# A third shifted copy made by two DMAs instead of VectorE, in a mixed attention and MLP kernel

## The chip, the cores and the metric

The kernel runs on one core of a Trainium2 chip. The metric is the device time of one execution in microseconds (us). TensorE multiplies matrices, ScalarE evaluates exponentials, VectorE does elementwise work, GpSimd is a further elementwise engine that can also issue DMAs, and SyncE (SP) issues nearly all DMAs. Each engine works through its own list of instructions in the order in which the program wrote them, and waits on semaphores for the others.

## The reference, cut to what matters

The input `x` is 2048 x 640 in bfloat16. It is layer-normed, and goes into two branches: attention with 32 heads of width 20, and an MLP that mixes along the sequence. The output is `x + attention * silu(mlp)`.

```python
xn = layernorm(x)
q, k, v = split_heads(xn @ wqkv)              # 32 heads, 20 wide
p = softmax(q @ k.T * 20 ** -0.5)             # 2048 x 2048 per head
s = merge_heads(p @ v) @ wo
u = gelu(einsum("bsd,sf->bdf", layernorm(xn), w1) + b1)
g = silu(transpose(einsum("bdf,fs->bds", u, w2) + b2))
out = x + s * g
```

Most of the work is in the scores: 32 heads x 4 blocks of 512 queries x 16 blocks of 128 keys make 2048 tiles of 128 x 512, and each needs an exponential and a product with `v`.

## The kernel before

**A planner writes every engine's program.** `Prog` keeps a list of tasks for each engine and a modelled time `T` for each. A task names the slots that it reads and writes; `Prog._add` derives from them the semaphore waits, and a modelled finish `fin`. The class `_Kern` runs a greedy loop over the engines: it asks each what it could do next (`pe_cands`, `eng_cands`), and appends the candidate that can start first. So the order on the chip is the order of the model, fixed when the program is built; on the chip nothing is reordered. DMAs go to SP in the order in which the planner emits them, over eight semaphores in rotation (`Prog.dma`).

**Scores.** Heads are taken in groups of four (`G`), and for each group the queries in blocks of 512 (`p`); a pair (G, p) is a pass `q`. A unit is one tile of scores, for one head and one block of keys. `emit_st` issues the score matmuls for up to four units at once, one in each 32-row part of TensorE (L1283). Two groups of three PSUM banks serve ScalarE, one further bank (`JB`) serves VectorE, and one (`AB`) accumulates the values. `do_st` can lend the last bank of a ScalarE group to VectorE when the modelled load of VectorE (`dve_load`) is below `LEND`.

**ScalarE's tiles.** `emit_exp` takes two or three banks through one activation, exp(scores), into `pt_sb` (L1313).

**VectorE's tiles.** VectorE makes an approximate exponential of the tiles of a *quad*: the four heads of a group for one block of keys. `emit_op1` adds a constant to the scaled scores, cuts at zero and writes the result as uint16 (L1324). These bits, read as bfloat16, are roughly 2 to the power of the score; the mantissa is linear between powers. Four such values, shifted by a quarter of a power each and weighted, average out most of the error. `emit_top` therefore makes three more copies of the finished quad, adding the integer constants `DK = (0, 32, 64, 96)` to the bits, each in one operation over 128 x 2048 elements:

```python
tk = pr.dve(lambda e: e.tensor_scalar(dst, src, dk, None, ALU.add), ...)   # L1362
```

The four versions are k = 0, 1, 2, 3; the first is the quad itself, in buffer `b0`. They live in `dt_sb`, eight buffers (`NTILE`) of 4 x 512 uint16 per partition; `tfree` lists the free ones, and at most three quads (`NLIVE`) are open at once. Only key blocks 0, 3, 6, 9 and 12 (`RC`) may become quads, because these have weighted values `vs_sb`, one set for each k over 0.

**Values.** `emit_pv` multiplies tiles with the values and accumulates (L1381). A ScalarE unit takes one matmul; a quad takes four for each k. Four heads run side by side in column parts of 32. Which of a quad's versions go next, and how many at once, is chosen in `pe_cands` (`PARTS` = (3, 1), or all that are there); a version's buffer goes back to `tfree` after its matmuls. `mk` lets a piece become a candidate 60 ns after the modelled finish of the last version that it reads.

**The rest.** Projections, the MLP and the output products are jobs whose matmuls fill TensorE's time between score groups (L648, L656, L965 and others). Where nothing fits, `emit_fill` issues matmuls with zeros (L1398).

Of the kernel before, what the change touches and what calls it, by code (L numbers as in the profile page):

```python
# [10 lines left out]
P = 128  # L11
# [28 lines left out]
class Prog:  # L40
# [2 lines left out]

    COMPUTE = ("pe", "act", "dve", "pool", "sp")
    LAT = {"pe": 55.0, "act": 55.0, "dve": 55.0, "pool": 80.0, "sp": 60.0}
    TAIL = {"pe": 170.0, "act": 118.0, "dve": 82.0, "pool": 60.0, "sp": 0.0}

    def __init__(self, nc, n_lanes=8):
        self.nc = nc
        self.n_lanes = n_lanes  # L50
        self.cengs = list(self.COMPUTE) + [f"d{i}" for i in range(n_lanes)]
# [8 lines left out]
        self.pipe = 0.0  # L60
        self.pe_end = 0.0
        self.low = 0
        self.lowt = 0.0
        self.alog = []
# [21 lines left out]
    def _add(self, eng, ceng, fn, reads, writes, name, extra_req=(), cost=100.0, tail=None):  # L86
        t = _Task(eng, ceng, fn, name)
        t.gidx = self.gcount
        self.gcount += 1
        self.tasks[eng].append(t)  # L90
        self.ctasks[ceng].append(t)
        t.cidx = len(self.ctasks[ceng])
        req = {}

        def need(tt):
            if tt is None:
                return
            if eng == "pe" and tt.ceng == "pe":
                return
            cur = req.get(tt.ceng)  # L100
            if cur is None or tt.cidx > cur.cidx:
                req[tt.ceng] = tt

        for s in reads:
            assert s.w is not None, f"read of uninit slot {s.name} by {name}"
            need(s.w)
        for s in writes:
            need(s.w)
            for r in s.readers.values():
                if r is not t:  # L110
                    need(r)
        for tt in extra_req:
            need(tt)
        start = self.T[eng]
        for tt in req.values():
            start = max(start, tt.fin + self.lat(eng, tt.ceng))
        kn = list(self.known[eng])
        for tt in sorted(req.values(), key=lambda x: -x.gidx):
            ci = self.cidx_of[tt.ceng]
            if kn[ci] >= tt.cidx:  # L120
                continue
# [12 lines left out]
        for s in writes:  # L134
            s.w = t
            s.readers = {}
        t.t0 = start
        if ceng not in self.COMPUTE:
            start = max(start, 700.0)
            if tail is not None:  # L140
                self.T[eng] = start + cost
                self.pipe = max(self.pipe, start) + cost
                t.fin = self.pipe - cost + tail
            else:
                self.T[eng] = start + 450.0
                self.pipe = max(self.pipe, start + 600.0) + cost
                t.fin = self.pipe + (1200.0 if self.pipe < 2500.0 else 2800.0 if cost > 800.0 else 1400.0)
        else:
            self.T[eng] = start + cost
            self.busy[eng] += cost  # L150
            t.fin = start + cost + (self.TAIL[eng] if tail is None else tail)
        return t
# [31 lines left out]
    def dma(self, fn, reads=(), writes=(), name="dma", lane=None, cost=3000.0, over=(), tail=None):  # L184
# [11 lines left out]
        t.need_inc = True  # L196
        return t

    def final_waits(self):
        for li in range(self.n_lanes):  # L200
            ceng = f"d{li}"
# [9 lines left out]
    def emit(self, sems):  # L211
# [12 lines left out]
        def make(engname):  # L224
            def body(eng):
                for t in self.tasks[engname]:
# [3 lines left out]
                    if t.fn is None:  # L230
                        continue
                    ins = t.fn(eng)
                    if engname == "sp" and t.ceng.startswith("d"):
# [32 lines left out]
class _Kern:  # L266
# [42 lines left out]
    QAT = (0.0, 0.0, 0.0, 0.0)  # L309
    ACTP = 30.0  # L310
    COLS = True
    NTILE, NLIVE, EARLY = 8, 3, True
    QC = ((0.5, 3.0), (3.2, 6.4), (9.0, 13.5), (14.0, 18.0), (19.0, 22.0))
    WIN = 16
    DON = True
    TOPP, EVP = 38.0, 36.0
    GROT = 1
    OPTS = (
        ("SLACK", (120.0, 40.0, 200.0, 320.0)),
        ("MINJ", (640.0, 320.0, 1000.0)),  # L320
        ("ROOM", (3, 6, 0)),
        ("DRIDE", (400.0, 150.0, 700.0)),
        ("LEND", (1800.0, 1300.0, 2400.0, 700.0, 0.0)),
        ("PARTS", ((2,), (2, 1), (3, 1), (1,), ())),
        ("LATE", (2.0, -9.0, 99.0)),
        ("DON", (True, False)),
        ("LONE", (False, True)),
        ("CONFL", (True, False)),
        ("TOPP", (38.0, 22.0)),
        ("EVP", (24.0, 36.0)),  # L330
        ("FGAP", (40.0, 150.0)),
        ("GROT", (1, 0)),
    )
    PLAN = ()
    PARTS = (3, 1)
# [17 lines left out]
    def build(self):  # L353
# [4 lines left out]
        with es:  # L358
# [19 lines left out]
            sb("dt_sb", [P, self.NTILE, 4, 512], u16)  # L378
# [13 lines left out]
            t["ps_all"] = E(nc.psum_tensor("ps_all", [P, 4096], f32))  # L392
            t["qk_dram"] = nc.dram_tensor("qk_scratch_dram", [2, 560, S], bf)
            t["oT_dram"] = nc.dram_tensor("oT_scratch_dram", [8 * P, S], bf)
            t["ok_dram"] = nc.dram_tensor("ok_scratch_dram", [S, 512], bf)
            sems = {}
            for e in ("pe", "act", "dve", "pool", "sp"):
                sems[e] = E(nc.semaphore(f"sem_{e}"))
            for i in range(pr.n_lanes):
                sems[f"d{i}"] = E(nc.semaphore(f"sem_d{i}"))  # L400
            self.t = t
            self.schedule()
            pr.final_waits()
# [7 lines left out]
    def schedule(self):  # L411
# [715 lines left out]
        avail = []  # L1127
        dquads = []
        tfree = list(range(self.NTILE))
        dlive = [0]  # L1130
        dop1 = []
        lent = set()
# [187 lines left out]
        def emit_op1():  # L1320
# [12 lines left out]
            if d["left"] == 0:  # L1333
                dtop.append([d, 1])
                d["fin"][0] = tk.fin
                if self.EARLY:
                    dquads.append((0.0, d))

        def emit_top():
            d, k = dtop[0]  # L1340
# [25 lines left out]
            dtop[0][1] += 1  # L1366
            for j in range(k, k + n):
                d["fin"][j] = tk.fin
            if k + n == 4:
                dtop.pop(0)  # L1370
                if not self.EARLY:
                    dquads.append((tk.fin, d))
                for j in range(2 if n == 2 else 1):
                    if d["pk"] > j:
# [37 lines left out]
        def emit_pv(items, quads):  # L1412
# [5 lines left out]
            freed = []  # L1418
            for d, n_ in quads:
                for k in range(d["pk"], d["pk"] + n_):  # L1420
                    for g in range(4):
                        seq.append(("d", d, k, g))
                    if k > (1 if self.MERGE else 0) or d["tl"][3] is not None:
# [16 lines left out]
            for i, s in enumerate(seq):  # L1440
# [15 lines left out]
                else:  # L1456
# [7 lines left out]
                    pt_busy[s0] = False  # L1464
                    avail.remove((fin, u, s0))
            tfree.extend(freed)
            for d in ends:
                dlive[0] -= 1
                dquads[:] = [x for x in dquads if x[1] is not d]
# [83 lines left out]
        for w in (1, 0):  # L1553
# [2 lines left out]
                       [S_("wkr" if w else "wqr")], f"wr{w}", 491520))  # L1556
        rw.append(("tag", "wr"))
        add_job("wr", rw, ("xTd15",), 30.0)
        add_job("bload", [
            ("dma", small(lambda e: e.dma_start(bload_sb[:, 0:FC], B_b1.rearrange("(fc p) -> p fc", p=P))), [], [S_("bl1")],  # L1560
             "dma_b1", 3000),
# [215 lines left out]
        def pe_cands(T):  # L1777
# [28 lines left out]
            if acc_ok[0] and pv_pass[0] < NP:  # L1806
# [29 lines left out]
                if quads:  # L1836
                    d0 = quads[0][1]
                    have = sum(f > 0.0 for f in d0["fin"])
                    left = have - d0["pk"]
                    whole = have == 4  # L1840
                    if left > 0 and whole:
                        if min(cnt) >= 1 or rem == len(pick):
                            pv.append(mk(pick, [(quads[0], left)]))
                            if len(pick) < rem or not pick:
                                pv.append(mk([], [(quads[0], left)]))
                        else:
                            pv.append(mk([], [(quads[0], left)]))
                    for n in self.PARTS:
                        if n < left or (n == left and not whole):
                            pv.append(mk([], [(quads[0], n)]))  # L1850
                if okp:
                    pv.append(mk(pick, []))
            jb = []
# [332 lines left out]
```

## Time and profile before

| | |
|---|---|
| median of 2 runs | 754.68 us (754.28 to 755.08) |
| the profiled execution, its own time | 754.1 us |
| its span, first to last instruction | 752.3 us |
| TensorE busy | 716.3 us (95%) |
| VectorE busy | 719.0 us (96%) |
| ScalarE busy | 730.0 us (97%) |
| GpSimd busy | 15.3 us (2%) |
| DMA queues, share of 16 engines | 23.4% + 0.8% + 0.1% |

In the profile's lines PE is TensorE (PEld its weight loads), ACT ScalarE, DVE VectorE, POOL GpSimd and SP SyncE; `L12` is a line of the kernel. A group's line gives what it writes and reads, the shape, the count, then the busy time and the mean of one in ns, and then the engine's idle time before these instructions with the engine that ended it. A row of digits shows 40 equal slices of the span, busy tenths in each. In a waits line the three numbers are us in total, times, and the longest. A timeline line starts with the start and the length in us. A windows line has the stretch, its length, the busy time of PE, PEld, DVE, ACT and POOL with counts, the granted clock, the DMA share and GB/s.

### The profile page before, as it was taken

How to read it: one execution, taken by the hardware profiler on the slowest of the kernel's cores; microseconds unless marked ns; L12 is line 12 of the kernel's file. 1: busy time of each engine (PE TensorE's matmuls, PEld its weight loads, DVE VectorE, ACT ScalarE, POOL GpSimd, SP SyncE). 2: the span in 40 equal slices, each digit the busy share in tenths (PEclk: the TensorE clock that was granted, in tenths of full speed). 3: DMA queues.
4: the chain of work that ended last, by engine and by line, in shares of the span. 5: the costliest groups of instructions: out<-in, count | busy, mean ns of one | idle time of the engine just before them, and what ended most of it. 6: DMA issues, size and time to landing. Idle time of an engine off the chain costs nothing.

```text
span 752.3 us, 23672 instructions
## 1 busy us (share of the span) xinstructions
PE 716.3 (95%) x10561; PEld 243.6 (32%) x10561; DVE 719.0 (96%) x1320; ACT 730.0 (97%) x707; POOL 15.3 (2%) x23
## 2 busy tenths in 40 slices
PE   9899999999999999999999999999999999999997
PEld 7332222222233232323223332323233332333233
DVE  7889999999999999999999999999999999999996
ACT  5989999999999999999999999999999999999995
POOL 4200000000000000000000000000000000000000
PEclk9999999999999999999999999999999999999999
DMA  8754111110121031212111131301325501041102
GB/s 237 155 110 48 56 38 37 20 38 5 38 62 20 13 76 31 72 24 69 20 38 21 30 87 24 74 13 29 79 76 81 128 28 51 7 152 47 47 15 70
DMA packets 119738, 42.66 MB, mean 57 GB/s; under 512 B 79172, under 2 KB 118468, under 8 KB 119588
## 3 DMA queue, kind: packets, MB, share of 16 engines
q1 hardware_dynamic: 119636, 41.15, 23.4%
q8 instruction: 82, 1.34, 0.8%
q14 instruction: 20, 0.16, 0.1%
HBM read 26.37 MB, written 10.22 MB: 49 GB/s over the span
## 4 chain that ended last, share of the span: by engine, by line
ACT 76%; PE 18%; DVE 6%; issue 0%; DVEq 0%
ACT pt_sb L1313 74%; PE ps_all L1381 5%; PE ps_all L1283 5%; PE ps_all L648 5%; DVE dt_sb L1324 1%; PE ps_all L1408 1%; ACT zt_sb L849 1%; DVE dt_sb L1362 1%; ACT zt_sb L844 1%; DVE bst_sb L532 1%; DVE bst_sb L530 1%; DVE regC L548 1%; PE ps_all L965 1%; PE ps_all L633 0%; DVE v_sb L1114 0%; PE ps_all L746 0%
## 5 line engine op out<-in xcount | busy, mean ns | idle before, releaser
L1313 ACT ACTIVATE pt_sb<-ps_all 128x1024 bf16<-128x1024 f32 (+1 forms) x681 | 711.2, 1242 | 4.9 <-PE ps_all L1283 2.1
L1324 DVE TENSOR_SCALAR dt_sb<-ps_all 128x512 uint16<-128x512 f32 x496 | 328.4, 683 | 15.9 <-PE ps_all L1283 8.9
L1283 PE MATMUL ps_all<-qk_sb 32*128 32x512 bf16 (+1 forms) x2128 | 269.1, 376 | 26.4 <-ACT pt_sb L1313 22.9
L1362 DVE TENSOR_SCALAR dt_sb<-dt_sb 128x2048 uint16<-128x2048 uint16 x372 | 241.2, 689 | 1.5
L1283 PEld LDWEIGHTS ps_all<-qk_sb 32*128 32x128 bf16 x2128 | 68.4, 91 | 280.9 <-ACT pt_sb L1313 226.4
L1381 PE MATMUL ps_all<-dt_sb,vs_sb 128*21 128x512 bf16 (+1 forms) x1536 | 130.7, 376 | 0.9 <-DVE dt_sb L1362 0.5
L1381 PE MATMUL ps_all<-pt_sb,v_sb 128*21 128x512 bf16 (+1 forms) x1616 | 127.0, 374 | 1.9 <-DVE v_sb L1114 0.9
L648 PE MATMUL ps_all<-regC,regA 128*32 128x128 bf16 (+1 forms) x1472 | 65.5, 297 | 0.0
L648 PE MATMUL ps_all<-regB,regA 128*32 128x128 bf16 (+1 forms) x1480 | 65.2, 298 | 0.3 <-DVE qs_sb L698 0.3
L1381 PEld LDWEIGHTS ps_all<-dt_sb,vs_sb 128*21 128x21 bf16 x1536 | 33.4, 90 | 51.7 <-issue 31.2
L1381 PE MATMUL ps_all<-dt_sb,v_sb 128*21 128x512 bf16 (+1 forms) x512 | 49.2, 377 | 0.1
L1381 PEld LDWEIGHTS ps_all<-pt_sb,v_sb 128*21 128x21 bf16 x1616 | 30.9, 90 | 49.2 <-issue 35.9
L648 PE MATMUL ps_all<-xnT_sb,wqk_sb 128*32 128x512 bf16 x640 | 46.1, 382 | 0.0
L648 PEld LDWEIGHTS ps_all<-regB,regA 128*32 128x32 bf16 x1480 | 27.4, 96 | 23.3 <-issue 10.9
L648 PEld LDWEIGHTS ps_all<-regC,regA 128*32 128x32 bf16 x1472 | 27.8, 96 | 22.0 <-issue 10.6
L965 PE MATMUL ps_all<-wv_sb,xnT_sb 128*128 128x512 bf16 (+1 forms) x160 | 27.3, 301 | 0.0
L656 PE MATMUL ps_all<-regC,regA 32*128 32x512 bf16 x64 | 24.6, 384 | 0.0
L648 PE MATMUL ps_all<-wv_sb,xnT_sb 128*32 128x480 bf16 x320 | 22.1, 369 | 0.3 <-DVE qs_sb L1117 0.3
L1505 DVE STREAM_TRANSPOSE tr_sb<-ps_all 128x512 f32<-128x512 f32 x31 | 22.0, 711 | 0.0
L656 PE MATMUL ps_all<-regB,regA 32*128 32x512 bf16 x56 | 21.5, 384 | 0.0
L1381 PEld LDWEIGHTS ps_all<-dt_sb,v_sb 128*21 128x21 bf16 x512 | 13.0, 90 | 20.6 <-issue 14.2
L1398 PE MATMUL ps_all<-wp_sb,zw_sb 128*21 128x512 bf16 (+1 forms) x244 | 19.4, 373 | 0.0
(88 smaller groups left out, 348.5 us busy)
## 6 DMA issues: line engine op xcount, KB each, us to landing
regA<-in_B_w_dram SPq DMA_DIRECT2D x6, 1024.0 KB
regA<-in_B_w_dram SPq DMA_DIRECT2D x8, 768.0 KB
qk_sb<-qk_scratch_dram SPq DMA_DIRECT2D x56, 80.0 KB
qk_scratch_dram<-qs_sb SPq DMA_DIRECT2D x32, 128.0 KB
regA<-in_A_x_dram SPq DMA_DIRECT2D x6, 640.0 KB
ok_scratch_dram<-on_sb SPq DMA_DIRECT2D x96, 20.0 KB
out_dram<-regC SPq DMA_DIRECT2D x3, 640.0 KB
wqk_sb<-in_A_wqkv_dram SPq DMA_DIRECT2D x2, 480.0 KB
```

What stands on the lines that cost most here:

```text
L530: steps.append(("dve", lambda e, b=b: e.bn_stats(bst_sb[:, b, 0:6], regA[:, b, 0:320]), [sx], [s0], f"{nm}s0", 393.0))
L532: steps.append(("dve", lambda e, b=b: e.bn_stats(bst_sb[:, b, 6:12], regA[:, b, 320:640]), [sx], [s1], f"{nm}s1", 393.0))
L648: fns.append(lambda e, c=c, e_=e_: e.matmul(oc(c, e_), lhsT[:, c:e_], rhs, start=start, stop=stop, tile_position=(0, c)))
L656: row = lambda g: (lambda e: e.matmul(oc(0, 128), lhsT[32 * g:32 * g + 32, :], rhs[32 * g:32 * g + 32, :], start=False, stop=False, tile_p ...
L965: steps.append(("pe", lambda e, c=c: e.matmul(ap, oT_sb[:, c, b * 128:(b + 1) * 128], wo_ap[:, c, c0:c0 + n], start=(opens and c == 0), st ...
L1283: t = pr.pe(lambda e, outp=outp, lhsT=lhsT, rhs=rhs, g=g: e.matmul(outp, lhsT, rhs, start=True, stop=True, tile_position=(32 * g, 0)), rea ...
L1313: tk = pr.act(lambda e: e.activation(outp, inp, AF.Exp, scale=math.log(2.0) / 128.0), reads=[bank_slot[b] for b in banks[:n]], writes=[S_( ...
L1324: tk = pr.dve(lambda e: e.tensor_scalar(w, src, WOFF, 0.0, ALU.add, ALU.max), reads=[bank_slot[bk]], writes=[S_(f"dt{d['tl'][0]}_{g}")], n ...
L1362: tk = pr.dve(lambda e: e.tensor_scalar(dst, src, dk, None, ALU.add), reads=[S_(f"dt{b}_{g}") for b in inb for g in range(4)], writes=[S_( ...
L1381: pr.pe(lambda e: e.matmul(outp, lhsT, rhs, start=(k == 0), stop=last, tile_position=(0, 32 * g)), reads=reads, writes=[bank_slot[AB]], na ...
L1398: pr.pe(lambda e, outp=outp, rhs=rhs, g=g: e.matmul(outp, zw_sb[:, 0:DH + 1], rhs, start=False, stop=False, tile_position=(0, 32 * g)), re ...
L1505: steps.append(("dve", lambda e: e.transpose(tr_sb[:, :], ps(AB)), [bank_slot[AB]], [S_("tr")], f"epT{q}", 632.0))
```

## The change

The eight buffers of `dt_sb` become six ordinary ones and two *x-buffers*. At the start GpSimd fills both with the constant 96 by memsets, and one of them is stored to a DRAM tensor, `kc_dram`. When the fourth first pass of a quad has been planned, `emit_x` looks for an x-buffer that will be ready no later than 3 us (`XWAIT`) after the quad. If there is one, GpSimd issues a DMA that adds the quad's bits (`b0`) to the constant in the x-buffer, which then holds version k = 3, and VectorE makes only k = 1 and 2. If there is none, VectorE makes all three as before. After the value matmuls have read the x-buffer, `refill` lets SP load the constant into it again from `kc_dram`.

The planner gets three lanes with semaphores for these DMAs (`NXL`), with modelled times: 1400 ns of issue on GpSimd, 2400 ns of transfer in which the DMAs follow one another, and 1600 ns to completion. When the first quad waits only for its x-buffer (k = 3), the value passes of the next quad may go ahead of it. With an x-buffer, `b0` is held until version 3 has been used. `OPTS` is only read through `PLAN`, which is empty.

```diff
+    NXL = 3
+    XISSUE, XMOVE, XTAIL = 1400.0, 2400.0, 1600.0
...
+        if eng == "pool" and ceng != "pool":
+            self.T[eng] = start + self.XISSUE
+            self.xpipe = max(self.xpipe, start + self.XISSUE) + self.XMOVE
+            t.fin = self.xpipe + self.XTAIL
...
+    def xdma(self, fn, reads, writes, name, lane):
+        ceng = f"x{lane}"
+        prev = self.ctasks[ceng][-1:]
+        t = self._add("pool", ceng, fn, reads, writes, name, extra_req=prev)
+        t.need_inc = True
+        return t
...
-    NTILE, NLIVE, EARLY = 8, 3, True
+    NTILE, NLIVE, EARLY = 6, 3, True
+    NX, XWAIT = 2, 3000.0
...
+        def emit_x(d, tk):
+            d["x"] = False
+            if not xfree:
+                return
+            x, b0 = xfree[0], d["tl"][0]
+            ws = [S_(f"dt{x}_{g}") for g in range(4)]
+            if max(pr.ready("pool", [], ws), pr.T["pool"]) > tk.fin + self.XWAIT:
+                return
+            xfree.pop(0)
+            d["x"] = True
+            d["tl"][3] = x
+            dst, src = dt_sb[:, x, :, :], dt_sb[:, b0, :, :]
+            t = pr.xdma(lambda e: e.dma_start(dst, src, accum_op=ALU.add), [S_(f"dt{b0}_{g}") for g in range(4)], ws,
+                        f"dX{d['q']}_{d['c']}", x - self.NTILE)
+            d["fin"][3] = t.fin
+            stats["x"] = stats.get("x", 0) + 1
+
+        def refill(x):
+            ws = [S_(f"dt{x}_{g}") for g in range(4)]
+            dst = dt_sb[:, x, :, :].rearrange("p a b -> p (a b)")
+            pr.dma(lambda e: e.dma_start(dst, kc_dram[:, :]), reads=[S_("kc")], writes=ws, name=f"kf{x}", cost=1320.0,
+                   tail=3000.0)
+            xfree.append(x)
...
-            if k + n == 4:
+            if k + n == (3 if d["x"] else 4):
...
-                quads = quads[:1]
+                quads = quads[:2 if quads and quads[0][1]["pk"] == 3 and quads[0][1].get("x") else 1]
...
-                x += (1730.0 if k == 1 else 1130.0) if self.MERGE else 600.0 * (4 - k)
+                x += (1730.0 if k == 1 else 1130.0) if self.MERGE else 600.0 * ((3 if d["x"] else 4) - k)
```

More of the change, by code (lines that the diff above doesn't have):

```diff
@@ L50, in __init__ @@
         self.n_lanes = n_lanes
-        self.cengs = list(self.COMPUTE) + [f"d{i}" for i in range(n_lanes)]
+        self.cengs = list(self.COMPUTE) + [f"d{i}" for i in range(n_lanes)] + [f"x{i}" for i in range(self.NXL)]
         self.cidx_of = {c: i for i, c in enumerate(self.cengs)}
@@ L60, in __init__ @@
         self.pipe = 0.0
+        self.xpipe = 0.0
         self.pe_end = 0.0
@@ L137, in _add @@
         t.t0 = start
-        if ceng not in self.COMPUTE:
+        if eng == "pool" and ceng != "pool":
+            self.T[eng] = start + self.XISSUE
+            self.xpipe = max(self.xpipe, start + self.XISSUE) + self.XMOVE
+            t.fin = self.xpipe + self.XTAIL
+        elif ceng not in self.COMPUTE:
             start = max(start, 700.0)
@@ L232, in body @@
                     ins = t.fn(eng)
-                    if engname == "sp" and t.ceng.startswith("d"):
+                    if t.ceng not in self.COMPUTE:
                         ins.then_inc(sems[t.ceng], 16)
@@ L318 @@
     OPTS = (
-        ("SLACK", (120.0, 40.0, 200.0, 320.0)),
+        ("SLACK", (0.0, 120.0, 40.0, 200.0, 320.0)),
         ("MINJ", (640.0, 320.0, 1000.0)),
-        ("ROOM", (3, 6, 0)),
+        ("ROOM", (6, 3, 0)),
         ("DRIDE", (400.0, 150.0, 700.0)),
         ("LEND", (1800.0, 1300.0, 2400.0, 700.0, 0.0)),
-        ("PARTS", ((2,), (2, 1), (3, 1), (1,), ())),
-        ("LATE", (2.0, -9.0, 99.0)),
+        ("PARTS", ((3, 1), (2,), (2, 1), (1,), ())),
+        ("LATE", (1.0, 2.0, -9.0, 99.0)),
         ("DON", (True, False)),
@@ L329 @@
         ("TOPP", (38.0, 22.0)),
-        ("EVP", (24.0, 36.0)),
-        ("FGAP", (40.0, 150.0)),
+        ("EVP", (36.0, 24.0)),
+        ("FGAP", (0.0, 40.0, 150.0)),
         ("GROT", (1, 0)),
+        ("JOBF", (4, 0, 8)),
     )
@@ L377, in build @@
             sb("pt_sb", [P, self.RP, 512], bf)
-            sb("dt_sb", [P, self.NTILE, 4, 512], u16)
+            sb("dt_sb", [P, self.NTILE + self.NX, 4, 512], u16)
             sb("zt_sb", [P, 2, 2, self.D], bf)
@@ L394, in build @@
             t["oT_dram"] = nc.dram_tensor("oT_scratch_dram", [8 * P, S], bf)
+            t["kc_dram"] = nc.dram_tensor("kc_scratch_dram", [P, 2048], u16)
             t["ok_dram"] = nc.dram_tensor("ok_scratch_dram", [S, 512], bf)
@@ L400, in build @@
                 sems[f"d{i}"] = E(nc.semaphore(f"sem_d{i}"))
+            for i in range(pr.NXL):
+                sems[f"x{i}"] = E(nc.semaphore(f"sem_x{i}"))
             self.t = t
@@ L1129, in schedule @@
         tfree = list(range(self.NTILE))
+        xfree = []
+        kc_dram = t["kc_dram"]
         dlive = [0]
@@ L1337, in emit_op1, with kc_steps @@
                     dquads.append((0.0, d))
+                emit_x(d, tk)
+        def emit_x(d, tk):
[20 more added lines that the diff above has]
+            xfree.append(x)
+        def kc_steps():
+            steps = []
+            for x in range(self.NTILE, self.NTILE + self.NX):
+                steps.append(("pool", lambda e, x=x: e.memset(dt_sb[:, x, :, :], int(self.DK[3])), [],
+                              [S_(f"dt{x}_{g}") for g in range(4)], f"kc{x}", 1500.0))
+            src = dt_sb[:, self.NTILE, :, :].rearrange("p a b -> p (a b)")
+            steps.append(("dma", lambda e: e.dma_start(kc_dram[:, :], src), [S_(f"dt{self.NTILE}_{g}") for g in range(4)],
+                          [S_("kc")], "kcst", 524288))
+            steps.append(("call", lambda: xfree.extend(range(self.NTILE, self.NTILE + self.NX))))
+            steps.append(("tag", "kc"))
+            return steps
         def emit_top():
@@ L1373, in emit_top @@
                 for j in range(2 if n == 2 else 1):
-                    if d["pk"] > j:
+                    if d["pk"] > j and not (d["x"] and d["pk"] < 4):
                         tfree.append(d["tl"][j])
@@ L1417, in emit_pv @@
             ends = [d for d, n_ in quads if d["pk"] + n_ == 4]
-            freed = []
+            freed, xs = [], []
             for d, n_ in quads:
@@ L1422, in emit_pv @@
                         seq.append(("d", d, k, g))
-                    if k > (1 if self.MERGE else 0) or d["tl"][3] is not None:
+                    if d.get("x"):
+                        if k in (1, 2):
+                            freed.append(d["tl"][k])
+                        elif k == 3:
+                            freed.append(d["tl"][0])
+                            xs.append(d["tl"][3])
+                    elif k > (1 if self.MERGE else 0) or d["tl"][3] is not None:
                         freed.append(d["tl"][k])
@@ L1466, in emit_pv @@
             tfree.extend(freed)
+            for x in xs:
+                refill(x)
             for d in ends:
@@ L1558, in schedule @@
         add_job("wr", rw, ("xTd15",), 30.0)
+        add_job("kc", kc_steps(), ("lnp14",), 43.0)
         add_job("bload", [
@@ L1835, in pe_cands @@
                 okp = bool(pick) and (min(cnt) >= 1 or len(pick) == rem or (tail and len(mine)))
-                if quads:
-                    d0 = quads[0][1]
-                    have = sum(f > 0.0 for f in d0["fin"])
+                for qd in quads:
+                    d0 = qd[1]
+                    have = next((i for i, f in enumerate(d0["fin"]) if f == 0.0), 4)
                     left = have - d0["pk"]
@@ L1842, in pe_cands @@
                         if min(cnt) >= 1 or rem == len(pick):
-                            pv.append(mk(pick, [(quads[0], left)]))
+                            pv.append(mk(pick, [(qd, left)]))
                             if len(pick) < rem or not pick:
-                                pv.append(mk([], [(quads[0], left)]))
+                                pv.append(mk([], [(qd, left)]))
                         else:
-                            pv.append(mk([], [(quads[0], left)]))
+                            pv.append(mk([], [(qd, left)]))
                     for n in self.PARTS:
                         if n < left or (n == left and not whole):
-                            pv.append(mk([], [(quads[0], n)]))
+                            pv.append(mk([], [(qd, n)]))
                 if okp:
```

## The prediction

> **What bounds the kernel now.** I read the page's busy shares, then the chain that ended last, then the costly groups, and then short stretches of the timeline, to price what changes hands. The shares and the 40 slices come first:
>
> ```profile
> PE 716.3 (95%) x10561; PEld 243.6 (32%) x10561; DVE 719.0 (96%) x1320; ACT 730.0 (97%) x707; POOL 15.3 (2%) x23
> ...
> DMA  8754111110121031212111131301325501041102
> ```
>
> Three engines are full at once; GpSimd and, after the start, the DMA engines have room. The chain and the groups say which of the three ends last:
>
> ```profile
> ACT 76%; PE 18%; DVE 6%; issue 0%; DVEq 0%
> ...
> L1313 ACT ACTIVATE pt_sb<-ps_all 128x1024 bf16<-128x1024 f32 (+1 forms) x681 | 711.2, 1242 | 4.9 <-PE ps_all L1283 2.1
> L1324 DVE TENSOR_SCALAR dt_sb<-ps_all 128x512 uint16<-128x512 f32 x496 | 328.4, 683 | 15.9 <-PE ps_all L1283 8.9
> ...
> L1362 DVE TENSOR_SCALAR dt_sb<-dt_sb 128x2048 uint16<-128x2048 uint16 x372 | 241.2, 689 | 1.5
> ```
>
> The chain runs along ScalarE's exponentials for most of the span, and ScalarE has only 4.9 us of idle time ahead of 681 of them. It does 2048 - 496 = 1552 score tiles in 711.2 us, 0.458 us each. VectorE does the other 496 tiles, 124 quads of four. The 372 copies (three a quad) are what the change acts on. Records of VectorE overlap a little, so I price by starts:
>
> ```profile
> 309.16 1.90 DVE L1362 TENSOR_SCALAR dt_sb<-dt_sb 128x2048 uint16<-128x2048 uint16 x3
> ...
> 310.96 1.29 DVE L1324 TENSOR_SCALAR dt_sb<-ps_all 128x512 uint16<-128x512 f32 x2
> ...
> 312.16 0.61 DVE L823 TENSOR_SCALAR zt_sb<-ps_all,b1h_sb 128x128 bf16<-128x128 f32 x2
> ```
>
> Three copies take 1.80 us from start to next start, 0.60 each; two first passes take 1.20, also 0.60 each. These three lines also show that copies come back to back directly after first passes.
>
> TensorE is in the same state. Its jobs are cut to fit between score groups:
>
> ```profile
> 304.53 0.83 PE L648 MATMUL ps_all<-xnT_sb,wqk_sb 128*32 128x512 bf16 x12
> ...
> 305.29 0.39 PE L1283 MATMUL ps_all<-qk_sb 32*128 32x512 bf16 x3
> ...
> 305.61 0.62 PE L648 MATMUL ps_all<-xnT_sb,wqk_sb 128*32 128x512 bf16 x8
> ...
> 306.16 0.39 PE L1283 MATMUL ps_all<-qk_sb 32*128 32x512 bf16 x3
> ```
>
> Twelve column matmuls occupy 0.76 us and eight 0.55, so four cost 0.21 us. A score group follows as soon as ScalarE frees its banks: there is no slack to speak of. Today TensorE seldom waits for a copy:
>
> ```profile
> PEld ps_all L1381 <- DVE dt_sb L1362: 12.2, 47, 0.6
> ```
>
> Last, how fast the DMA engines move wide rows. A 1 MB weight load is issued at 311.97 us, its bytes flow from about 313.2, and in this stretch and a heavy one at the start the windows show:
>
> ```profile
> 313.00:317.00 4.00, 3.97 (x60) 1.18 (x56) 3.96 (x7) 4.00 (x4) 0.00 (x0) 1.00 0.97 264
> ...
> 9.00:14.00 5.00, 4.91 (x59) 3.98 (x57) 4.64 (x16) 3.63 (x6) 0.69 (x1) 1.00 1.05 360
> ```
>
> The last two columns are the DMA share and GB/s. Divided, they give 272 and 343 GB/s with the engines full.
>
> **What the Trainium skill says.** "SBUF — State Buffer", section "SBUF: two separate sides", says that a GpSimd DMA has its descriptors written by GpSimd through a port pair that VectorE holds during its two-port fast modes; its next section prices one case, about 620 ns alone and 3100 beside such an operation. Before has no GpSimd DMA, so no run here shows it yet; the copy, four times the elements of a first pass in the same 0.60 us, is clearly in a fast mode. "Collectives: The Full Stack", section "The bandwidth ceiling: the fold count and why AG ≠ RS ≠ AR", says that a DMA that adds reads two sources and reached half the rate of a copy. "DMA: Bandwidth & Descriptors", section "Issuing engines are not separate DMA queues", says that all queues run on the same 16 engines and interleave. The shares over 1 and 264 GB/s above agree that one load can fill them.
>
> **The change, part by part.** Sums are made against the profiled execution's own 754.1 us (span 752.3, so 1.8 around it); the median of the runs is 754.68, 0.6 higher.
>
> *How often it applies.* A quad comes every 5.7 us (some 700 us of attention over 124). The planner's loop for one of the two constant-filled buffers is 1.4 + 2.4 + 1.6 = 5.4 us for the adding DMA, about 1 us until its matmuls run, and 3.0 us for the refill: 9.4 us, or one buffer per 4.7. So most quads get one. SP's queue refuses some: its 16 transposes hold it for 22 us near 567. I take 110 copies of 124.
>
> *VectorE.* It loses 110 x 0.60 = 66 us. The planner hands tiles over while VectorE's load is low, so the gain is shared. A quad moved from ScalarE costs VectorE six operations, 3.6 us, and saves ScalarE 4 x 0.458 = 1.83 us. Equal relief is at 66 / (3.6 + 1.83) = 12.2 quads, worth 22 us.
>
> *TensorE.* A quad on VectorE has four value passes against one, 3 x 0.21 = 0.63 us more: 8 us for 12 quads. To end 22 us sooner it must find 30 us. It has 752.3 - 716.3 = 36 us idle, and 61 sets of filler matmuls (L1398, 244 in all) of which some can go. That is barely enough, so I count 18 of the 22 us. Six ordinary buffers in place of eight serve the same two quads, because one with an x-buffer needs three; I cost that at nothing while the x-buffers come back in time.
>
> *The DMA engines.* Before uses 23.4 + 0.8 + 0.1 = 24.3% of them, 183 us. A refill is 524,288 bytes: 1.5 us at 343 GB/s, 1.9 at 272. The addition is two reads: 2.4 us as the code plans, 3.1 to 3.9 at twice the refill. For 110 of each that is 429 to 638 us more, in all 612 to 821 us of a 750 us span, or 82 to 109%. The low end works; the high end is a bound of its own. In either, bursts collide.
>
> *The new wait.* The fourth value pass on TensorE (k=3) waits for the DMA, and TensorE runs in written order: behind the waiting weight load stand the next score groups and so ScalarE. The code lets another quad's passes go ahead of it, but that order is fixed by planned times. The real latency is bounded by parts: descriptors 1.0 (the skill's first-byte price for such DMAs, in the DMA page's "Specifications") to 1.4 (the plan); a lock-out by copies that follow the first passes 0 to 1.3 (two at 0.60); the move 2.4 to 3.9; completion 1.0 to 1.6; queueing behind a refill or a weight load 0 to 2. The ends are 4.4 and 10.2 us; I take 7.0, as one or two of these bite each time. Planned are 5.4. Value passes come some 0.6 to 1.1 us after their copies in the stretch above (four at 307.35 after a copy that ended at 306.26; four at 310.47 after one that ended at 309.85), so 1.0 of the 1.6 us is absorbed, and about 0.5 us a quad is left once ScalarE's banks in hand are counted: 110 x 0.5 = 55 us. Nothing wins that back, because all three engines shift together.
>
> *The rest.* GpSimd gains two memsets (the 1280-wide one takes 1.16 us, so some 2 us each) and one store, at the start, hidden: GpSimd is 2% busy. About 110 refills go to SP, 0.4 us of issue each; loads of keys and queries and stores of outputs stand behind a refill that waits for TensorE. They have a lead of several us, so I cost them at nothing; without the cover each could add up to a microsecond at 31 pass ends. The reordered option lists do nothing, as the plan that indexes them is empty.
>
> Sum: 754.1 - 18 + 55 = 791.1 us, and 0.6 more for the median: **792 us**.
>
> **The rivals.**
>
> *DMAs land in time* (the other side). Latency stays under 6.4 us, the planner's 5.4 and the lag, and the balance gives its 18 us: 754.7 - 18 = 736.7, some 732 with a little more coverage. For it: DMA is at 0.18 or so in the middle of the span, and 4.4 us is possible. Against: 82% load at best. It decides if stalls average under (18 - 15) / 110 = 0.03 us a quad, since 2% is 15 us; with an occasional late one it is at the edge.
>
> *Even.* Stalls of 0.03 to 0.3 us a quad, or so few buffers ready that the planner falls back on the VectorE copy in most quads, and the change hardly happens: 740 to 770 us. For it: the plan itself refuses a buffer that is over 3 us late. Against: the loop's 4.7 us beside 5.7.
>
> *DMA saturation or lock-out as the new bound.* At 109% load, or with GpSimd holding the shared port for 1.4 us against each quad's two copies, stalls reach 1.2 us a quad: 754.7 - 18 + 132 = 869 us. For it: the 264 GB/s row. Against: 4 KB rows are wider than those of that load.
>
> **How the numbers follow.** A measurement of this kernel can tell about 2% from no change, 739.6 to 769.8 us. Late additions with 0.3 to 0.9 us of stall (769 to 835 us, point 792): 0.37. Saturation or lock-out above that: 0.15. Even: 0.20. In time: 0.28. So faster 0.28, same 0.20, slower 0.52. The range has to hold cases of both signs: from 731, which leaves out some 0.05 of the fast case, to 865, which leaves out half of the saturated one: 0.12 to 0.13 in all. The likeliest case's own range is 769 to 835.
>
> **What would show it.** Right: waits of TensorE's L1381 loads, now for a DMA and some 50 us in total; ScalarE's idle time ahead of its exponentials growing from 4.9 us to tens; DMA share above 0.7 in mid-span; some 300 copies (three for each of 136 quads, less 110) in place of 372, and first passes up from 496 to about 540. Wrong: DMA waits of under 10 us and ScalarE still without gaps would mean that the additions land in time, and the time falls towards 737. VectorE copies far longer than 0.69 us, or a long wait of VectorE with free inputs, would show that the port lock and not the transfer costs the time. Over 350 copies still on VectorE would mean that the change hardly applied.

## The result and the profile after

The changed kernel takes 902.75 us (median of 2 runs, 901.62 to 903.89) against 754.68: the ratio is 1.1962, interval 1.1892 to 1.2032. The profiled execution is the one of 901.62 us; its span is 899.8. From the page, the shares come first, then the slices of the DMA engines, the queues, the chain and the groups:

```profile
PE 770.0 (86%) x10619; PEld 249.0 (28%) x10629; DVE 699.9 (78%) x1259; ACT 731.7 (81%) x709; POOL 116.0 (13%) x128
...
DMA  9678777776776668778877667678795766748873
...
q1 hardware_dynamic: 134612, 95.69, 39.2%
q0 software_dynamic: 14832, 54.01, 33.0%
...
PE 34%; DMA 32%; DVE 17%; ACT 13%; issue 3%; SPq 1%; POOL 0%; POOLq 0%; DVEq 0%
...
L1334 ACT ACTIVATE pt_sb<-ps_all 128x1024 bf16<-128x1024 f32 (+1 forms) x683 | 711.4, 1161 | 131.1 <-PE ps_all L1304 114.6
L1345 DVE TENSOR_SCALAR dt_sb<-ps_all 128x512 uint16<-128x512 f32 x520 | 345.6, 680 | 130.3 <-PE ps_all L1304 115.7
...
L1439 PE MATMUL ps_all<-dt_sb,vs_sb 128*21 128x512 bf16 (+1 forms) x1608 | 148.5, 403 | 86.8 <-DMA dt_sb<-dt_sb 85.2
L1420 DVE TENSOR_SCALAR dt_sb<-dt_sb 128x2048 uint16<-128x2048 uint16 x287 | 192.1, 691 | 6.3 <-PE ps_all L1439 4.4
```

No engine is full any more. ScalarE works as long as before (731.7 us against 730.0) but stands idle for 131.1 us ahead of its exponentials, where it was 4.9; VectorE has the same hole, 130.3. Both end it with a score group of TensorE (L1304, which was L1283). The chain no longer runs along ScalarE: DMAs hold 32% of it, 23% the additions and 7% the refills. The additions are queue q0: 103 of them, in 33.0% of the DMA engines' time. VectorE has 85 fewer copies at an almost unchanged 691 ns (689 before), and 24 more first passes (520 for 496), which is six quads taken over from ScalarE.

What held GpSimd and TensorE stands in the waits (us in total, times, longest):

```profile
POOL dt_sb L1373 <- DMA dt_sb<-kc_scratch_dram: 211.3, 28, 18.6
...
PEld ps_all L1439 <- DMA dt_sb<-dt_sb: 100.0, 45, 5.8
```

The weight loads of the value passes (L1439, which was L1381) wait 100.0 us for an addition, and their matmuls 85.2 us. It is not every addition that is a little late: 45 of 103 are, by 2.2 us each on average. GpSimd, which issues the additions, waits 211.3 us for refills, but that is not behind most of the late ones: by the trace, 12 of the 45, with 30.1 of the 100.0 us, were issued when a refill had landed, and 32 when VectorE had finished something. On average these 45 took 6.5 us to land, and TensorE stood ready for them 4.3 us after their issue, where the code plans at least 5.4. So half of the 2.2 us is a landing that took longer than planned, and half an issue that came late against TensorE. One case with a refill, on the chain:

```profile
296.54 4.84 DMA dt_sb<-kc_scratch_dram
301.38 0.02 issue
301.40 0.02 POOLq L243
301.42 0.49 issue
301.91 7.83 DMA dt_sb<-dt_sb
309.74 0.04 issue
309.78 1.46 PE ps_all L1439 x11
```

TensorE finishes with an x-buffer at 296.54; its refill takes 4.84 us to land; only then can GpSimd issue the next addition into it, which lands 7.83 us later. From the end of one use to the start of the next it is 13.2 us, where the code plans 3.0 for the refill and 5.4 for the addition, 8.4. TensorE's matmuls stop from 305.5 to 309.78, and then this window follows (busy of PE, PEld, DVE, ACT and POOL with counts, clock, DMA share, GB/s):

```profile
309.80:314.00 4.20, 4.20 (x37) 0.90 (x37) 1.72 (x3) 2.05 (x2) 0.08 (x1) 0.60 0.41 129
```

After four idle microseconds TensorE has 0.60 of its clock in this window. The Trainium skill says so ("TensorE: Matmul & The Clock Gate", section "HAM oscillation — how this bites in real kernels": a wait for a DMA that outlasts the activity window makes the next piece start at the lower clock), and the trace agrees. Over the whole span the granted clock is 0.928, where it was 0.999, and TensorE is busy 53.7 us longer with 58 more matmuls. So a stall is followed by some microseconds in which TensorE is slower. For one kernel below only the faster of two executions is used, because the other had a lower granted clock and took 13 us longer.

### The profile page after: what moved, and what is told of

Read it like the earlier page. It is cut to its first block, busy times and chain, and to the rows that moved or that the text cites. A ratio compares the mean times of both kernels' runs of the same rounds, so it can differ in the third digit from the quotient of the medians.

```text
span 899.8 us, 24093 instructions
## 1 busy us (share of the span) xinstructions
PE 770.0 (86%) x10619; PEld 249.0 (28%) x10629; DVE 699.9 (78%) x1259; ACT 731.7 (81%) x709; POOL 116.0 (13%) x128
## 3 DMA queue, kind: packets, MB, share of 16 engines
q0 software_dynamic: 14832, 54.01, 33.0%
## 4 chain that ended last, share of the span: by engine, by line
PE 34%; DMA 32%; DVE 17%; ACT 13%; issue 3%; SPq 1%; POOL 0%; POOLq 0%; DVEq 0%
DMA dt_sb<-dt_sb 23%; ACT pt_sb L1334 12%; PE ps_all L1439 12%; PE ps_all L1304 10%; PE ps_all L667 8%; DVE dt_sb L1345 7%; DMA dt_sb<-kc_scratch_dram 7%; DVE dt_sb L1420 4%; PE ps_all L984 2%; DVE tr_sb L1571 1%; PE ps_all L1456 1%; DVE regC L567 1%; DVE regC L999 1%; DVE v_sb L1133 1%; DMA regA<-in_A_x_dram 1%
## 5 line engine op out<-in xcount | busy, mean ns | idle before, releaser
L1334 ACT ACTIVATE pt_sb<-ps_all 128x1024 bf16<-128x1024 f32 (+1 forms) x683 | 711.4, 1161 | 131.1 <-PE ps_all L1304 114.6
L1345 DVE TENSOR_SCALAR dt_sb<-ps_all 128x512 uint16<-128x512 f32 x520 | 345.6, 680 | 130.3 <-PE ps_all L1304 115.7
L1304 PE MATMUL ps_all<-qk_sb 32*128 32x512 bf16 (+1 forms) x2128 | 281.1, 396 | 20.0 <-ACT pt_sb L1334 18.2
L1439 PE MATMUL ps_all<-dt_sb,vs_sb 128*21 128x512 bf16 (+1 forms) x1608 | 148.5, 403 | 86.8 <-DMA dt_sb<-dt_sb 85.2
L1420 DVE TENSOR_SCALAR dt_sb<-dt_sb 128x2048 uint16<-128x2048 uint16 x287 | 192.1, 691 | 6.3 <-PE ps_all L1439 4.4
L1373 POOL DMA_DIRECT2D dt_sb<-dt_sb x103 | 97.1, 943 | 737.2 <-DVE dt_sb L1345 423.2
L1304 PEld LDWEIGHTS ps_all<-qk_sb 32*128 32x128 bf16 x2128 | 68.6, 91 | 292.5 <-ACT pt_sb L1334 180.5
L1439 PE MATMUL ps_all<-pt_sb,v_sb 128*21 128x512 bf16 (+1 forms) x1592 | 133.7, 397 | 5.5 <-DVE v_sb L1133 4.2
L1439 PEld LDWEIGHTS ps_all<-dt_sb,vs_sb 128*21 128x21 bf16 x1608 | 36.5, 92 | 152.6 <-DMA dt_sb<-dt_sb 100.0
L1439 PE MATMUL ps_all<-dt_sb,v_sb 128*21 128x512 bf16 (+1 forms) x536 | 54.8, 401 | 1.6 <-DVE tr_sb L1571 1.5
L667 PE MATMUL ps_all<-xnT_sb,wqk_sb 128*32 128x512 bf16 x640 | 51.7, 403 | 0.2 <-DVE qs_sb L1136 0.2
L1439 PEld LDWEIGHTS ps_all<-pt_sb,v_sb 128*21 128x21 bf16 x1592 | 31.0, 92 | 57.8 <-issue 40.9
L675 PE MATMUL ps_all<-regC,regA 32*128 32x512 bf16 x80 | 31.4, 393 | 0.0
L984 PE MATMUL ps_all<-wv_sb,xnT_sb 128*128 128x128 bf16 (+1 forms) x153 | 25.6, 303 | 6.2 <-DVE regC L999 4.3
L1456 PE MATMUL ps_all<-wp_sb,zw_sb 128*21 128x512 bf16 x240 | 22.2, 411 | 0.0
L1439 PEld LDWEIGHTS ps_all<-dt_sb,v_sb 128*21 128x21 bf16 x536 | 13.6, 91 | 24.2 <-issue 15.8
```

The costliest lines, as they stand in the source:

```text
L667: fns.append(lambda e, c=c, e_=e_: e.matmul(oc(c, e_), lhsT[:, c:e_], rhs, start=start, stop=stop, tile_position=(0, c)))
L675: row = lambda g: (lambda e: e.matmul(oc(0, 128), lhsT[32 * g:32 * g + 32, :], rhs[32 * g:32 * g + 32, :], start=False, stop=False, tile_p ...
L984: steps.append(("pe", lambda e, c=c: e.matmul(ap, oT_sb[:, c, b * 128:(b + 1) * 128], wo_ap[:, c, c0:c0 + n], start=(opens and c == 0), st ...
L1304: t = pr.pe(lambda e, outp=outp, lhsT=lhsT, rhs=rhs, g=g: e.matmul(outp, lhsT, rhs, start=True, stop=True, tile_position=(32 * g, 0)), rea ...
L1334: tk = pr.act(lambda e: e.activation(outp, inp, AF.Exp, scale=math.log(2.0) / 128.0), reads=[bank_slot[b] for b in banks[:n]], writes=[S_( ...
L1345: tk = pr.dve(lambda e: e.tensor_scalar(w, src, WOFF, 0.0, ALU.add, ALU.max), reads=[bank_slot[bk]], writes=[S_(f"dt{d['tl'][0]}_{g}")], n ...
```

## The experiments

Each ratio is against the kernel before on the same chip, whose medians there were 753.85 to 754.31 us.

### Both transfers cut to 16 bytes a partition

The first theory was that late DMAs make the difference, and neither VectorE nor the order does. Keeping the order and all semaphores and shrinking only the bytes separates these.

```diff
-e.dma_start(dst, src, accum_op=ALU.add)
+e.dma_start(dst[:, 0, 0:8], src[:, 0, 0:8], accum_op=ALU.add)
-e.dma_start(dst, kc_dram[:, :])
+e.dma_start(dst[:, 0:8], kc_dram[:, 0:8])
```

> All instructions, their order and all waits as after; the adding DMA and the refill move only 16 bytes a partition, so that version k=3 is left mostly unwritten. Theory A (DMAs land later than the order was written for, and TensorE waits in order, after which its granted clock falls): no DMA wait of over 10 us in total is left, the clock is back above 0.99, and the time is 740 to 770 us. Theory B (the order itself, with six ordinary buffers, is bad, or GpSimd's issue disturbs VectorE): still over 830 us. If my 18 us of balance gain was right, 737.

Measured: 779.74 us, ratio 1.0336 (1.0306 to 1.0366). An addition now lands 2.4 us after its issue (median). TensorE's waits for it, in this kernel:

```profile
PEld ps_all L1439 <- DMA dt_sb<-dt_sb: 4.9, 5, 1.3
```

So 902.75 - 779.74 = 123.0 us come from the size of the transfers, and 779.74 - 754.31 = 25.4 us come from what is left, with the copies nearly free. That second number is a surprise: the order alone is slower than before, and the time lies 10 us above the range of theory A. One DMA wait of over 10 us is left too: GpSimd still waits 47.0 us for refills.

### One of the two cut

The next three kernels cut only the addition; only the refill; and turn the addition into a plain copy.

```diff
# the addition alone
+e.dma_start(dst[:, 0, 0:8], src[:, 0, 0:8], accum_op=ALU.add)
# the refill alone (the whole addition then takes its source from kc_dram)
+e.dma_start(dst.rearrange("p a b -> p (a b)"), kc_dram[:, :], accum_op=ALU.add)
+e.dma_start(dst[:, 0:8], kc_dram[:, 0:8])
# plain copy, refill whole
+e.dma_start(dst, src)
```

> As after, but only the adding DMA is cut to 16 bytes a partition (k=3 left mostly unwritten); the refill is whole. Theory A with the addition as its main part: 0.33 of DMA time goes, landing falls from 5.7 to about 2.5 us, and the time comes within 20 us of the kernel with both cut. A second theory, that the refill's lateness (4.4 to 6.9 us on the chain against 3.0 planned) is the larger part: most of the 148 us stays, over 830 us.

> As after, but the refill is cut to 16 bytes a partition, and the addition, whole in size, takes the constant in DRAM as its source, so that k=3 holds other values. Addition as the main part: the time stays over 820 us, TensorE still waits 60 us or more for it. Refill as the main part: under 780 us. Half each: 790 to 820.

> As after, but the GpSimd DMA copies the quad and adds nothing (k=3 equals k=0); all sizes, order and waits as after. If the read of the destination is what makes the addition long: its queue's share falls from 33% to about 18%, landing from 5.7 to about 4.2 us, and the time to 790 to 830. If GpSimd's issue and the fixed latency make it: little change, over 870.

| addition | refill | us | ratio |
|---|---|---|---|
| whole | whole | 902.75 | 1.1962 (1.1892 to 1.2032) |
| whole, from DRAM | 16 B | 858.38 | |
| plain copy | whole | 813.83 | 1.0788 (1.0757 to 1.0819) |
| 16 B | whole | 786.46 | 1.0425 (1.0376 to 1.0474) |
| 16 B | 16 B | 779.74 | 1.0336 (1.0306 to 1.0366) |

All three times lie where the addition as the main part puts them. The row of 858.38 us is a single execution, so its ratio has no interval.

The refill alone costs 6.7 us (786.46 - 779.74), the addition alone 78.6 (858.38 - 779.74, with the reservation that its source is another memory). Together they cost 123.0, so some 38 us are left for their interaction. They share the loop of a buffer and the DMA engines; no run tells which of the two it is. That the DMA adds and doesn't just copy is worth 902.75 - 813.83 = 88.9 us. The plain copy, in the page and in the waits:

```profile
q0 software_dynamic: 14832, 54.01, 17.7%
```

```profile
PEld ps_all L1439 <- DMA dt_sb<-dt_sb: 31.5, 22, 4.3
```

The bytes on the queue are the same, 54.01 MB. Per transfer it is 17.7% of 812.1 us over 103, 1.40 us of all 16 engines; the addition is 33.0% of 899.8 over 103, 2.88 us, 2.06 times as much. Landing takes 3.8 us in the median against 5.7.

### Where the 25 us come from: six buffers

The kernel before with six buffers for quads in place of eight, and no x-buffers:

```diff
-    NTILE, NLIVE, EARLY = 8, 3, True
+    NTILE, NLIVE, EARLY = 6, 3, True
+    NX = 0
```

> Before with six ordinary buffers in place of eight, no x-buffer and no added DMA; VectorE makes all copies. My step that six cost nothing: 750 to 758 us. If the buffers are what costs the 25 us of the order (the kernel with both DMAs cut took 779.7): 770 to 785.

Measured: 761.19 us, 1.01 (1.0085 to 1.0115), 7.3 us above before. This lies between the two ranges: six buffers do cost something, but less than a third of the 25 us. First passes fall to 484: with fewer buffers free the planner gives VectorE fewer quads, and ScalarE more.

### Realistic times for the planner

If lateness against the plan is the matter, and not the transfers as such, the same transfers must do little harm once the plan knows their times.

```diff
-    XISSUE, XMOVE, XTAIL = 1400.0, 2400.0, 1600.0
+    XISSUE, XMOVE, XTAIL = 900.0, 2900.0, 3600.0
-    NX, XWAIT = 2, 3000.0
+    NX, XWAIT, FTAIL = 2, 0.0, 4500.0     # FTAIL: the refill's tail, was 3000
```

A second kernel has a refill tail of 6000 and the MLP's parameter `MLP_B` at 20.0 in place of 24.0.

> The change with the planner told later times, near those measured: issue 900, transfer 2900, completion 3600 ns for the addition (7.4 us in place of 5.4), refill 4500 in place of 3000, and an x-buffer is used only when ready as the quad is; it then uses 77 of them. Theory A (the order is written for DMAs that come too early): waits of TensorE for the addition fall from about 100 us to under 25, the clock is above 0.98, the time 745 to 775 us. Rival (the DMA engines are saturated, so that later times only move the collision): DMA waits stay over 60 us, over 820 us.

> As the run with later times, with the refill told 6000 ns and the MLP's jobs asked for earlier (20 in place of 24), which uses 66 x-buffers. Theory A: waits for the addition under 15 us, and the time at best that of before, 742 to 765 us, because TensorE has little room for more value passes. Rival: over 800.

Measured: 771.07 us, 1.0233 (1.0215 to 1.0252), with 77 additions; and 763.75 us, 1.0125 (1.0105 to 1.0144), with 66. Both lie in the ranges of theory A. The second kernel's value passes:

```profile
L1439 PE MATMUL ps_all<-dt_sb,vs_sb 128*21 128x512 bf16 (+1 forms) x1560 | 133.7, 377 | 6.3 <-DMA dt_sb<-dt_sb 4.1
```

Landing is hardly faster than in the changed kernel (medians 5.6 and 5.4 us against 5.7), yet TensorE's matmuls wait 9.1 and 4.1 us for it instead of 85.2, and the clock is back at 0.99. The damage is lateness against a fixed order, and not the load on the DMA engines as such. There are also fewer additions, so a part of this is that the change is made less often: 0.83 us of wait an addition at first (85.2 / 103), then 0.12 and 0.06.

The order of the second kernel with both transfers cut to 16 bytes shows what its transfers still cost:

> The order of the run with the latest times (66 additions, 763.8 us), with both DMAs cut to 16 bytes a partition (k=3 mostly unwritten). If late landing is what keeps that order above before: 745 to 752 us. If the order and the six buffers keep it there: 758 to 764.

Measured: 756.87 us, 1.0039 (1.0031 to 1.0047). This is between the two ranges, so each theory holds in part: the transfers cost 6.9 us, and the rest of the order is 2.9 us above before.

### The refill without a DMA

GpSimd fills the x-buffer itself, which takes the refills out of the DMA engines:

```diff
-            pr.dma(lambda e: e.dma_start(dst, kc_dram[:, :]), ..., cost=1320.0, tail=3000.0)
+            pr.pool(lambda e: e.memset(dt_sb[:, x, :, :], int(self.DK[3])), ..., cost=1850.0)
-    XISSUE, XMOVE, XTAIL = 1400.0, 2400.0, 1600.0
+    XISSUE, XMOVE, XTAIL = 900.0, 2400.0, 2600.0
```

> The constant is written again by a GpSimd memset (1.8 us in the trace of after) in place of the refill DMA; completion told 2600 ns. The refill's DMA load (1.7 us of all engines, 103 times) and its latency go. Theory A: DMA share about 0.5, landing about 5 us, 780 to 830 us. If GpSimd's memset and VectorE's copies lock each other out of a shared port: copies well over 0.69 us on the mean, and 850 or more.

Measured: 845.98 us, 1.1223 (1.1183 to 1.1263), with 116 additions. The time is just below the 850 of the lock and outside the range of theory A; the copies decide. The groups:

```profile
L1380 POOL MEMSET dt_sb<- 128x2048 uint16 x116 | 217.2, 1873 | 237.3 <-PE ps_all L1437 237.3
L1418 DVE TENSOR_SCALAR dt_sb<-dt_sb 128x2048 uint16<-128x2048 uint16 x286 | 245.5, 878 | 1.8 <-PE ps_all L1437 0.6
```

The copies take 878 ns on average instead of 691, though their median is still 682; single ones take up to 2.5 us. VectorE holds 45% of this kernel's chain. The trace tells which: the 93 copies beside a memset take 1282 ns on average, the other 193 take 683. So a lock between GpSimd and VectorE exists, but it is the memset that takes it. The issue of an adding DMA hardly lengthens VectorE's copies: 691 ns on average in the changed kernel, 689 before.

### The start: memsets beside VectorE

The prediction had the two memsets at the start as hidden. The changed kernel's timeline shows them beside VectorE:

```profile
29.10 3.55 POOL L1388 MEMSET dt_sb<- 128x2048 uint16 x2
...
29.19 3.99 DVE L567 TENSOR_SCALAR regC<-regA,st_sb 128x640 bf16<-128x640 bf16 x2 [0.48 <-POOL st_sb L563]
...
33.63 1.04 PE L1439 MATMUL ps_all<-pt_sb,v_sb 128*21 128x512 bf16 x8 [2.55 <-DVE v_sb L1133]
```

Two layer-norm operations that take 0.80 us as a pair elsewhere take 3.99 beside the memsets; TensorE waits 2.55 us, and its clock is 0.66 from 30 to 40 us. The last kernel keeps the order of the one with 756.87 us and writes the same bytes as 32-bit words, half as many elements:

```diff
-e.memset(dt_sb[:, x, :, :], int(self.DK[3]))
+e.memset(dt_sb[:, x, :, :].bitcast(mybir.dt.uint32), int(self.DK[3]) * 65537)
```

> The kernel with the later times and both transfers cut to 16 bytes a partition, its order unchanged, but the two start fills of GpSimd written as 1024 words of 32 bits in place of 2048 of 16 (same bytes). In the versions with two filled buffers two memsets of GpSimd take 3.55 us at 28 to 33 us, and the two layer-norm operations of VectorE beside them take 3.99 us in place of 0.80; TensorE then waits 2.55 us and runs at a granted clock of 0.57 to 0.66 until 40 us. Theory (the memsets keep VectorE from its fast two-port reads and writes of SBUF, for as long as they run): the memsets take about 1.8 us, the two VectorE operations about 2.2 us, and the kernel ends 1.5 to 4 us sooner than 756.87, so 753 to 755.5. Rival (VectorE was held by something else there, or the start has slack): the memsets are shorter, the two VectorE operations still about 4 us or the end unchanged at 756.5 to 757.5.

Measured: 752.11 us, 0.9979 (0.9971 to 0.9987), 4.8 us less than 756.87, which is somewhat more than the 1.5 to 4 expected. VectorE's part of the start in this kernel's timeline:

```profile
27.90 1.84 POOL L1388 MEMSET dt_sb<- 128x1024 uint32 x2
...
27.99 2.28 DVE L567 TENSOR_SCALAR regC<-regA,st_sb 128x640 bf16<-128x640 bf16 x2 [0.48 <-POOL st_sb L563]
```

VectorE is released with the memsets, 1.7 us sooner. The clock from 30 to 40 us is 1.00, where it was 0.57 in the kernel with 756.87 us; that is the likely source of the rest of the 4.8, but no run separates the two. The Trainium skill ("SBUF — State Buffer", section "SBUF: two separate sides") says that the shared port pair is an exclusive lock, held for a whole instruction by whichever engine starts first. Both timelines agree: the first memset starts 0.09 us before VectorE's first operation, and that operation, in both, ends 0.2 us after the second memset.

### The ceiling, and a smaller change

How much could the third copy bring if it cost nothing? Here k = 3 reads the quad itself, with eight buffers and no DMA. Two parameters of the planner differ as well (`LEND` is 1300 and `PARTS` is (2, 1)):

```diff
-            d["tl"][3] = x          # and the addition
+            d["tl"][3] = d["tl"][0]
+            d["fin"][3] = tk.fin
```

> The third copy costs nothing at all: no DMA, no x-buffer, eight ordinary buffers, VectorE makes two copies and the matmuls of k=3 read the quad itself (so that k=3 holds k=0's values). The planner lends at a load of 1300 ns and takes value passes in pieces of two or one. It bounds what the change could have brought. My balance (18 to 22 us): 732 to 737 us. If TensorE has no room for more value passes: 742 to 752.

Measured: 745.8 us, 0.9884 (0.9857 to 0.991), 8.2 us less than before.

```profile
PE 708.1 (95%) x10505; PEld 240.8 (32%) x10505; DVE 675.1 (91%) x1226; ACT 721.9 (97%) x706; POOL 15.3 (2%) x23
```

VectorE has room (91%), ScalarE is 97% busy. The planner moves only five quads (516 first passes for 496) though nearly a third of the copies is gone (258 for 372). TensorE is idle for 36 us of the span, as before. That fits the range given for a TensorE without room, but whether TensorE or the planner's own rules keep it at five quads isn't shown.

A smaller change has one x-buffer and seven others, with additions planned at 900, 2900 and 5000 ns, a refill tail of 5000 and `MLP_B` at 22.0:

> Seven ordinary buffers and one x-buffer, the planner told 900, 2900 and 5000 ns for the addition and 5000 for the refill: about 40 additions. If cost goes with the number of additions (103: 903 us, 77: 771, 66: 764): 752 to 760 us, no gain. If few, well-timed additions pay: under 750.

Measured: 759.22 us, 1.0063 (1.0043 to 1.0083), with 40 additions. None of the versions that make the third copy in full by DMA is faster than the kernel before.

## Why the prediction was right or wrong

Slower was right, and so was the way: an addition lands late, TensorE waits for it in its written order, ScalarE starves behind. The kernel would have been slower without that too, by the 25 us of its order, which the prediction had as a gain of 18. The size was wrong: 792 us forecast, 902.75 measured, outside the range of 731 to 865. Of the 111 us missing, 68 belong to one term of the sum and 43 to the other.

**The term of +55 us measured 123.** The number of additions was nearly right, 103 for 110; the stall of 0.5 us each was 1.2 (123.0 / 103). Its parts, one by one:

- The latency of 7.0 us was too long: it is 5.7 in the median, inside the two ends of 4.4 and 10.2 (lowest 4.5, highest 10.7). The doubled engine time of an addition is confirmed, 2.88 us against 1.40; it was 2.4 to 3.9 in the prediction.
- The step that failed is the absorption: "1.0 of the 1.6 us is absorbed, and about 0.5 us a quad is left". It subtracts one typical lag from one typical delay. With the 5.7 us that were measured, against 5.4 planned, it would leave no stall at all, and yet 1.2 us an addition were lost. In its place the trace shows a spread on both sides. TensorE waited for none of 58 additions, and for each of the other 45 by 2.2 us: they landed 6.5 us after their issue, and TensorE was ready after 4.3, so that the lag which was to absorb a delay was itself short by 1.1 us. With later times in the plan, waits of this kind nearly go.
- The buffer's loop is a part of it: "I cost that at nothing while the x-buffers come back in time". They don't; GpSimd waits 211.3 us for refills. But only 12 of the 45 late additions had just been held by a refill, 30.1 of the 100.0 us. Why the issue of the other 33 came late against TensorE isn't shown, nor that the 38 us of interaction come from the loop.
- The drop of the clock after each stall was left out. On TensorE's own account, the 121.2 us between the spans of the changed kernel (899.8) and of the one with small transfers (778.6) are 78.4 us of idle time and 42.8 us of busy time, 770.0 against 727.2, for the same work. So about a third of the cost is work at the lower clock. This is an account of one engine's time; no run takes the clock away from the stalls.

**The term of -18 us measured +25.** The balance gain was 8.2 us even with a free copy. The rule "66 / (3.6 + 1.83) = 12.2 quads" supposes that the planner hands over all that VectorE gains; it handed over six in the changed kernel and five in the free one. And three costs that the prediction put at nothing or left out stand against the gain:

- Six buffers in place of eight, "at nothing": 7.3 us.
- The memsets, "at the start, hidden: GpSimd is 2% busy": at least 4.8 us in the one order in which this was measured, since the shorter memsets are still there. GpSimd's own idle time hid nothing here, because VectorE stood while its memsets ran.
- The end. In the kernel with small transfers, and then in the kernel before, the last 48 us look like this. ScalarE is busy for 22.47 and for 39.58 of them:

```profile
730.00:778.00 48.00, 38.82 (x507) 17.80 (x503) 35.35 (x70) 22.47 (x21) 4.96 (x5) 1.00 0.21 61
```

```profile
704.00:752.00 48.00, 41.58 (x609) 17.20 (x601) 41.98 (x80) 39.58 (x36) 1.15 (x1) 0.99 0.15 52
```

  The kernel with 756.87 us has 39.56. So the first order keeps some 17 us of work of other engines for the end, where few exponentials are left to run beside it. The changed kernel and the others that keep its order end in the same way (18 to 22 us), and those that plan 7.4 us or more for an addition don't (37 to 39). Why the planner leaves this work for the end isn't known.

As a rough sum, 7.3 + 4.8 - 8.2 = 3.9 us, near the 2.9 us of the order with 66 additions, which has no such end. With the 17 us it makes 21 of the 25. This is worked out from different orders, and no run removes the end alone.

**The signs named beforehand.** Right ones: waits for a DMA by the value passes (some 50 us expected, 100.0 found), ScalarE's idle time in the tens (131.1), a DMA share above 0.7 in the middle (0.73 from 100 to 850 us), some 300 copies (287). First passes were to rise to 540 and rose to 520.

**The rivals.** "In time" and "even" fell with the result. "Saturation or lock-out" has the size of the stall, 1.2 us a quad, but neither of its causes: the DMA engines are at 73% and not at 109%, and the copies on VectorE did not get longer. Its 869 us still carried the 18 us of gain. A lock-out did touch GpSimd, but little: an issue beside a copy takes 984 ns on average (65 of them), any other 871. The load itself was forecast well: 656 us of DMA time (72.9% of 899.8) lie inside the 612 to 821 that the prediction had. A load that fits was no guarantee that each transfer is in time.

## What to carry to other kernels

Work moved off a full engine onto a DMA is worth only what the next full engine can hand over, here 8.2 us of 755 as this planner orders it; find that ceiling with a version in which the work is free before building the transfer. In a program whose order is fixed ahead, price a transfer by how late each one is against the plan, its buffer's whole loop included, and not by its mean latency. The stall after which the clock was looked at, of some four microseconds, was paid again in TensorE's clock. An idle GpSimd was not free for a memset while VectorE ran its copies.

## What the runs showed of the hardware that I had not expected

- A DMA of 512 KB that adds to its destination takes 2.88 us of the 16 engines and lands in 5.7 us; the plain copy of the same bytes takes 1.40 and 3.8. GpSimd's issue of it takes 869 ns in the median against 540.
- The same addition with 2 KB in all still lands only after 2.0 to 2.4 us (lowest and median). By these medians some 2.4 of the 5.7 us of the whole one don't come from its bytes (an estimate).
- GpSimd's memset of 128 x 2048 takes 1.81 us as 16-bit elements and 0.96 as half as many 32-bit words, with the same bytes. VectorE's operation that starts beside two of them takes 3.64 and 1.93 us, where it takes 0.44 elsewhere.
